# Output rows four to a partition in an attention and gated-convolution kernel, stored as 112 and 15 partitions

## The chip, the cores and the metric

The kernel runs on one core of a Trainium2 chip. The metric is the device time of one execution in microseconds. The engines are named as in the profile: PE (TensorE matmul), PEld (TensorE weight load, the loading of the matmul's stationary operand), DVE (VectorE), ACT (ScalarE), POOL (GpSimd) and SP (SyncE, which issues DMAs). DMAs are issued from the queues of SP and ACT.

## The reference

Two stages, with B = 4, N = 6336 and C = 256, in float32. q and k are normalised over N, the scores are channel by channel, and the result goes through a causal convolution of five taps, a sigmoid and two matrix products:

```python
qn = q / (norm(q, axis=1) + 1e-6);  kn = k / (norm(k, axis=1) + 1e-6)
s = kn.transpose(0, 2, 1) @ qn / tau          # 256 x 256 per batch
a = exp(s - s.max(-1)); a /= a.sum(-1) + 1e-9
x = v @ a                                     # 6336 x 256 per batch
gate_pre = sum(conv_w[k] * xp[:, k:k + S] for k in range(5))   # xp: x with four zero rows ahead
gate = 1 / (1 + exp(-gate_pre))
out = (gate * (x @ w_val)) @ w_out
```

## The kernel before

Per batch there is a score pass and a chunk pass. The score pass reads q and k in 17 groups of up to three rows per partition and accumulates the 256 x 256 scores (`score_group`, matmuls at line 242). Its weights are every second channel of a row (`dealt`: channels are dealt to two halves, so neighbours in a weight load lie two floats apart). Rows with index below `nw` go as plain float32 in one product; the others are split into a high and a low part (`hi`) and go as three faster products. The softmax (`softmax`, a generator run in small steps between other work) turns the scores into the weights `w` of two products: `a`, and `a` times `w_val`.

The chunk pass takes 12 chunks of 508 rows and one of 240 (`chunks`; `all_steps` are the 52 pairs of batch and chunk). For each chunk, v is loaded, transposed by DVE and split (`load_v`, `turn_v`, `cast_v`, `low_v`), then:

- `conv`: x, transposed (channels on partitions), by matmuls at line 401 into `x_ps`, and five taps on ACT and DVE into `gate`;
- `sigmoid`, then `value`: the value product at line 401 into `val_ps`, multiplied into `gate`;
- `split_g`: `gate` into a high and a low part, `g_hi` and `g_lo`, tiles of 128 channels x 2 halves x 508 rows in float32;
- `finish`, run one step later: the output product at line 468. The gate is the stationary operand (its columns are the chunk's rows) and `w_out` the moving one, 256 columns wide. For each block of up to 128 rows six matmuls (two channel halves by three products) accumulate in half a PSUM bank. ACT copies a bank with two blocks to `o_sb` (line 478) and two DMAs store the chunk.

Before the change, block j of a chunk is the rows j x 128 to j x 128 + 127, the last block starting at w - 128, so that it overlaps the one before it by four rows (by 16 in the chunk of 240). Partition p of block j holds row j x 128 + p, so each stored piece is one row of 1 KB.

```python
o_ps[:, u * C:(u + 1) * C], gs[:, h, off:off + P], ws[:, h, :]      # line 468: out, weights, moving
store.dma_start(out=out[b, t0:t0 + full * P].rearrange("(j p) c -> p j c", p=P), in_=o_sb[:, 0:full, :])
```

The stores go out on ACT's queue, those of the last chunk but one on SP's. For the very last chunk `finish` copies its two blocks one by one, on ACT and on DVE, and stores each from its own queue (lines 474 and 476). `o_sb` has two buffers in the pool `w_p`. The tiles of q and k (`raw`) have six buffers in the pool `raw_p`.

The order of the work is written out by hand in the main loop (a step runs score groups, convolution, value product, split and the finish of the step before), with `behind(...)` and `tc.issue_after` for fine places. Within that, the framework's scheduler orders each engine's instructions by a simulated timeline; it also places the waits.

Of the kernel before, what the change touches and what calls it, by code (L numbers as in the profile page):

```python
# [9 lines left out]
F32 = mybir.dt.float32  # L10
# [8 lines left out]
P = 128  # L19
# [11 lines left out]
def kernel(  # L31
# [13 lines left out]
    nc = tc.nc  # L45
    B, N, C = q.shape
# [6 lines left out]
    raw_p = ctx.enter_context(tc.tile_pool(name="raw_p", bufs=6))  # L53
# [5 lines left out]
    w_p = ctx.enter_context(tc.tile_pool(name="w_p", bufs=2))  # L59
# [5 lines left out]
    first = RP % GROUP or GROUP  # L65
# [274 lines left out]
    NT = -(-(HALO + WMAX) // P)  # L340
# [99 lines left out]
    def split_g(b, i):  # L440
# [11 lines left out]
            nc.gpsimd.tensor_tensor(gl[:, :, 0:w], gate[:, :, 0:w], gh[:, :, 0:w].bitcast(F32), ALU.subtract)  # L452
        gts[b, i] = (gh, gl)

    def finish(b, i):
        t0, w = chunks[i]
        gh, gl = gts.pop((b, i))
        nt = -(-w // P)
        offs = [min(j * P, w - P) for j in range(nt)]
        o_sb = w_p.tile([P, NT, C], F32, name="o_sb")  # L460
        for j in range(0, nt, 2):
            pair = offs[j:j + 2]
            o_ps = ps.tile([P, 512], F32, name="o_ps", tag="bank")
            for u, off in enumerate(pair):
                n_ = 0
                for h in range(NH):
                    for gs, ws in ((gh, wo_hi), (gh, wo_lo), (gl, wo_hi)):
                        nc.tensor.matmul(o_ps[:, u * C:(u + 1) * C], gs[:, h, off:off + P], ws[:, h, :],  # L468
                                         start=n_ == 0, stop=n_ == 3 * NH - 1)
                        n_ += 1  # L470
            if (b, i) == all_steps[-1]:

                for u, (copy, dma) in enumerate(((nc.scalar.copy, nc.scalar), (nc.vector.tensor_copy, nc.sync))[:len(pair)]):
                    copy(o_sb[:, j + u, :], o_ps[:, u * C:(u + 1) * C])
                    first = max((j + u) * P - pair[u], 0)
                    dma.dma_start(out=out[b, t0 + pair[u] + first:t0 + pair[u] + P], in_=o_sb[first:P, j + u, :])
                continue
            marks["ACT"] = nc.scalar.copy(o_sb[:, j:j + len(pair), :], o_ps[:, 0:len(pair) * C].rearrange("p (j c) -> p j c", c=C))
        if (b, i) == all_steps[-1]:
            return  # L480
        full = w // P
        store = nc.sync if (b, i) == all_steps[-2] else nc.scalar
        store.dma_start(out=out[b, t0:t0 + full * P].rearrange("(j p) c -> p j c", p=P), in_=o_sb[:, 0:full, :])
        if w % P:
            store.dma_start(out=out[b, t0 + full * P:t0 + w], in_=o_sb[P - w % P:P, full, :])


    all_groups = [(b, g) for b in range(B) for g in range(NG)]
    all_steps = [(b, i) for b in range(B) for i in range(NC)]
# [5 lines left out]
    marks = {}  # L495
# [125 lines left out]
    for n in range(len(all_steps)):  # L621
# [39 lines left out]
        if prev:  # L661
            with behind(*{len(all_steps) - 2: ["CONV"], len(all_steps) - 1: ["G"]}.get(n, [])):
                finish(*prev)
    finish(*all_steps[-1])


# [30 lines left out]
```

## Time and profile before

| | |
|---|---|
| time, three runs | 619.65, 622.12, 622.36 us (median 622.12) |
| profiled execution | 620.85 us, span 619.0 us |
| mean granted TensorE clock | 0.993 |
| PE busy | 599.0 us (97%) |
| DVE, POOL, ACT busy | 498.1, 489.7, 469.3 us |
| output product (line 468) | 1,200 matmuls, 1,200 weight loads |
| stores | 104 DMAs, 50 + 50 of them (lines 483 and 485) on ACT's queue |

A page of the profile gives the busy time of each engine, the span in 40 slices, the DMA queues, the chain of work that ended last, and the costliest groups of instructions. A group's row has its line, engine and operation, what it writes and reads, the count, the busy time, the mean length of one in ns, and the idle time ahead of it with what ended it. Matmuls are pipelined: one of 256 columns is shown as 280 ns long, while the next starts much sooner, so that their pace is to be read from the starts, or from the chain's pieces (start, length, line, count). A weight load overlaps the matmul before it.

### The profile page before, as it was taken

Reading aid. Unit: us, or ns where it says so; the run is one execution under the profiler, and the core shown is the slowest. Engines: PE = TensorE matmul, PEld = TensorE weight load, DVE = VectorE, ACT = ScalarE, POOL = GpSimd, SP = SyncE. Lnnn points to the kernel's source line nnn. Section 1 sums busy time; section 2 is a strip of 40 time slices with the busy share of each in tenths; the row PEclk is TensorE's granted clock in tenths of the full one; section 3 lists DMA queues with packets and bytes.
Section 4 is the critical chain, followed back from the end, with each engine's and each line's share of the span. In section 5 each row is a group of like instructions: output and inputs, shape, how many; then the busy total and the mean of one; then the engine's idle time right before and its main releaser. Section 6 shows DMA issues by size and latency. Waiting matters only on the chain.

```text
span 619.0 us, 10261 instructions
## 1 busy us (share of the span) xinstructions
PE 599.0 (97%) x3596; PEld 537.3 (87%) x3596; DVE 498.1 (80%) x763; ACT 469.3 (76%) x576; POOL 489.7 (79%) x261
## 2 busy tenths in 40 slices
PE   8998999898999999999999999999999999999996
PEld 7987888787898998999989999898898888888895
DVE  3885689778788879889887887988887998988782
ACT  5567868486779896877868987787868876877763
POOL 2776798699787699998986699998986486877842
PEclk9997999999999999999999999999999999999999
DMA  8999996475464666765664767665143245552113
GB/s 278 401 275 320 236 286 189 141 189 177 143 189 143 190 185 176 214 186 151 187 179 140 198 169 219 166 216 136 51 99 106 69 120 135 130 140 83 64 45 116
DMA packets 154596, 105.80 MB, mean 171 GB/s; under 512 B 110768, under 2 KB 137648, under 8 KB 154544
## 3 DMA queue, kind: packets, MB, share of 16 engines
q1 hardware_dynamic: 128768, 79.82, 46.5%
q10 hardware_dynamic: 25776, 25.32, 13.5%
q8 instruction: 28, 0.46, 0.3%
q14 instruction: 24, 0.20, 0.1%
HBM read 79.16 MB, written 25.95 MB: 170 GB/s over the span
## 4 chain that ended last, share of the span: by engine, by line
PE 71%; DMA 12%; ACT 5%; POOL 4%; issue 4%; DVE 2%; SPq 2%; ACTq 0%; POOLq 0%; DVEq 0%
PE o_ps L468 19%; PE val_ps L401 18%; PE x_ps L401 18%; PE s_ps L242 14%; DMA v_raw<-in_v_dram 4%; DMA raw<-in_q_dram 2%; DMA raw<-in_k_dram 2%; DMA out_dram<-o_sb 2%; POOL v_lo L385 2%; DMA w_raw<-in_moe_w_val_dram 1%; PE o_ps L328 1%; DVE gate L421 1%; POOL acc L217 1%; SPq L365 1%; SPq L76 1%
## 5 line engine op out<-in xcount | busy, mean ns | idle before, releaser
L421 DVE SCALAR_TENSOR_TENSOR gate<-x_ps,wa,gate 128x508 f32<-128x508 f32 (+1 forms) x400 | 268.6, 715 | 14.0 <-ACT gate L418 11.3
L385 POOL TENSOR_TENSOR v_lo<-v_raw,v_hi 128x1024 fp32r<-128x1024 f32 (+1 forms) x52 | 123.7, 2380 | 45.0 <-ACT v_hi L379 44.7
L201 POOL TENSOR_TENSOR hi<-raw,hi 128x1536 fp32r<-128x1536 f32 (+3 forms) x51 | 142.5, 2797 | 20.0 <-ACT hi L200 13.5
L401 PE MATMUL x_ps<-v_hi,w 128*128 128x512 f32 (+1 forms) x416 | 140.7, 388 | 5.6 <-DVE gate L421 5.6
L401 PE MATMUL val_ps<-v_hi,w 128*128 128x508 f32 (+1 forms) x416 | 134.2, 382 | 0.0
L452 POOL TENSOR_TENSOR g_lo<-gate,g_hi 128x1016 fp32r<-128x1016 f32 (+1 forms) x50 | 118.6, 2372 | 15.1 <-ACT g_hi L451 12.1
L217 DVE TENSOR_TENSOR acc_ps<-acc_ps,sq 128x512 f32<-128x512 f32 (+1 forms) x124 | 85.8, 692 | 37.8 <-ACT sq L214 35.6
L468 PE MATMUL o_ps<-wo_hi,g_hi 128*128 128x256 f32 x400 | 112.9, 285 | 0.0
L468 PE MATMUL o_ps<-wo_lo,g_hi 128*128 128x256 f32 x400 | 111.4, 281 | 0.0
L214 ACT ACTIVATE sq<-raw 128x1536 f32<-128x1536 f32 (+3 forms) x69 | 96.2, 1396 | 17.4 <-DMA raw<-in_k_dram 14.0
L217 POOL TENSOR_TENSOR acc<-acc,sq 128x512 f32<-128x512 f32 x68 | 88.7, 1305 | 25.6 <-ACT sq L214 24.4
L468 PE MATMUL o_ps<-wo_hi,g_lo 128*128 128x256 f32 x400 | 107.7, 282 | 1.1 <-POOL g_lo L452 1.1
L242 PE MATMUL s_ps<-hi 128*128 128x256 f32 (+1 forms) x714 | 97.7, 286 | 0.0
L401 PEld LDWEIGHTS x_ps<-v_hi,w 128*128 128x128 f32 x416 | 77.1, 188 | 20.1 <-issue 6.2
L242 PEld LDWEIGHTS s_ps<-hi 128*128 128x128 f32 (+1 forms) x714 | 92.1, 196 | 2.5
L401 PEld LDWEIGHTS val_ps<-v_hi,w 128*128 128x128 f32 x416 | 77.1, 188 | 13.5
L373 DVE STREAM_TRANSPOSE v_raw<-v_raw 128x1024 f32<-128x1024 f32 (+1 forms) x52 | 62.3, 1200 | 31.3 <-DMA v_raw<-in_v_dram 27.7
L418 ACT ACTIVATE gate<-x_ps,wa 128x508 f32<-128x508 f32 (+1 forms) x104 | 68.1, 666 | 21.4 <-PE x_ps L401 20.6
L438 DVE TENSOR_TENSOR gate<-val_ps,gate 128x508 f32<-128x508 f32 (+1 forms) x104 | 65.3, 654 | 20.8 <-ACT gate L431 10.5
L242 PE MATMUL s_ps<-raw 128*128 128x256 f32 (+1 forms) x324 | 79.2, 391 | 0.7 <-DMA raw<-in_k_dram 0.7
L401 PE MATMUL x_ps<-v_lo,w 128*128 128x512 f32 (+1 forms) x208 | 79.8, 384 | 0.0
L401 PE MATMUL val_ps<-v_lo,w 128*128 128x508 f32 (+1 forms) x208 | 79.0, 380 | 0.0
(81 smaller groups left out, 811.1 us busy)
## 6 DMA issues: line engine op xcount, KB each, us to landing
raw<-in_q_dram SPq DMA_DIRECT2D x64, 384.0 KB
raw<-in_k_dram SPq DMA_DIRECT2D x64, 384.0 KB
v_raw<-in_v_dram SPq DMA_DIRECT2D x176, 128.0 KB
out_dram<-o_sb ACTq DMA_DIRECT2D x47, 384.0 KB
out_dram<-o_sb ACTq DMA_DIRECT2D x47, 124.0 KB
v_raw<-in_v_dram SPq DMA_DIRECT2D x16, 120.0 KB
v_raw<-in_v_dram SPq DMA_DIRECT2D x16, 64.0 KB
raw<-in_q_dram SPq DMA_DIRECT2D x4, 128.0 KB
```

The source lines that it names most:

```text
L201: marks["POOL"] = nc.gpsimd.tensor_tensor(hi[r, js, :, 1, :], raw[r, js, :, :], hi[r, js, :, 0, :].bitcast(F32), ALU.subtract)
L214: marks["SQ"] = nc.scalar.activation(sq[0:np_, ja:jb], raw[0:np_, ja:jb], AF.Square)
L217: marks["DVE" if key == "acc" else "POOL"] = eng.tensor_tensor(st[key][0:np_], st[key][0:np_], sq[0:np_, j], ALU.add)
L242: marks["PE"] = nc.tensor.matmul(st["s"][:, h, :], lhs, rhs, start=False, stop=stop and h == NH - 1 and n_ == len(ops) - 1)
L373: marks["T"] = nc.vector.transpose(t, t)
L385: nc.gpsimd.tensor_tensor(tl[:, :, 0:g, :], vraw.pop((b, i)), th[:, :, 0:g, :].bitcast(F32), ALU.subtract)
L401: marks["PRODUCT"] = nc.tensor.matmul(ps, wt[:, which, ws, ch, hs], vs[:, ch, lo:hi_], start=n_ == 0, stop=n_ == 3 * NH - 1)
L418: nc.scalar.activation(gate[:, h, 0:w], x_ps[:, 0:w], AF.Copy, scale=cw[:, h, 0:1])
L421: marks["TAP"] = nc.vector.scalar_tensor_tensor(gate[:, h, 0:w], x_ps[:, tap:tap + w], cw[:, h, tap:tap + 1], gate[:, h, 0:w], ALU.mult, A ...
L438: nc.vector.tensor_tensor(gate[:, h, 0:w], val_ps[:, 0:w], gate[:, h, 0:w], ALU.mult)
L452: nc.gpsimd.tensor_tensor(gl[:, :, 0:w], gate[:, :, 0:w], gh[:, :, 0:w].bitcast(F32), ALU.subtract)
L468: nc.tensor.matmul(o_ps[:, u * C:(u + 1) * C], gs[:, h, off:off + P], ws[:, h, :], start=n_ == 0, stop=n_ == 3 * NH - 1)
```

## The change

Row r x nt + j of a chunk now goes to partition r of block j, with nt = 4 blocks (2 in the chunk of 240) of 127 (120) rows. The weights of line 468 are therefore every nt-th float of the gate. A partition's four rows lie one behind the other in the output, so that a stored piece is 4 KB, and blocks no longer overlap. `even` splits a store into the largest multiple of 16 partitions and the rest: 112 and 15, or 112 and 8. The very last chunk's copies go to tiles of the pool `raw_p` under the tag of q and k instead of `o_sb`, and each of its two blocks is stored by two DMAs in pieces of 1 KB.

```diff
+    def even(rows):
+        whole_ = rows // 16 * 16
+        return [x for x in ((0, whole_), (whole_, rows)) if x[0] < x[1]]
+
     def finish(b, i):
         t0, w = chunks[i]
         gh, gl = gts.pop((b, i))
         nt = -(-w // P)
-        offs = [min(j * P, w - P) for j in range(nt)]
-        o_sb = w_p.tile([P, NT, C], F32, name="o_sb")
+        rows = w // nt
+        at_end = (b, i) == all_steps[-1]
+        if not at_end:
+            o_sb = w_p.tile([P, NT, C], F32, name="o_sb")
         for j in range(0, nt, 2):
-            pair = offs[j:j + 2]
+            pair = range(j, min(j + 2, nt))
             o_ps = ps.tile([P, 512], F32, name="o_ps", tag="bank")
-            for u, off in enumerate(pair):
+            for u in range(len(pair)):
                 n_ = 0
                 for h in range(NH):
                     for gs, ws in ((gh, wo_hi), (gh, wo_lo), (gl, wo_hi)):
-                        nc.tensor.matmul(o_ps[:, u * C:(u + 1) * C], gs[:, h, off:off + P], ws[:, h, :],
+                        turn = gs[:, h, 0:w].rearrange("p (r j) -> p j r", j=nt)[:, j + u, :]
+                        nc.tensor.matmul(o_ps[0:rows, u * C:(u + 1) * C], turn, ws[:, h, :],
                                          start=n_ == 0, stop=n_ == 3 * NH - 1)
                         n_ += 1
-            if (b, i) == all_steps[-1]:
+            dst = out[b, t0:t0 + w].rearrange("(r j) c -> r j c", j=nt)
+            if at_end:
                 for u, (copy, dma) in enumerate(((nc.scalar.copy, nc.scalar), (nc.vector.tensor_copy, nc.sync))[:len(pair)]):
-                    copy(o_sb[:, j + u, :], o_ps[:, u * C:(u + 1) * C])
-                    first = max((j + u) * P - pair[u], 0)
-                    dma.dma_start(out=out[b, t0 + pair[u] + first:t0 + pair[u] + P], in_=o_sb[first:P, j + u, :])
+                    o_end = raw_p.tile([P, C], F32, name="o_end", tag="raw")
+                    copy(o_end[0:rows], o_ps[0:rows, u * C:(u + 1) * C])
+                    for r0, r1 in even(rows):
+                        dma.dma_start(out=dst[r0:r1, j + u, :], in_=o_end[r0:r1])
                 continue
-            marks["ACT"] = nc.scalar.copy(o_sb[:, j:j + len(pair), :], ...)
+            marks["ACT"] = nc.scalar.copy(o_sb[0:rows, j:j + len(pair), :], ...)
...
-        full = w // P
         store = nc.sync if (b, i) == all_steps[-2] else nc.scalar
-        store.dma_start(out=out[b, t0:t0 + full * P].rearrange("(j p) c -> p j c", p=P), in_=o_sb[:, 0:full, :])
-        if w % P:
-            store.dma_start(out=out[b, t0 + full * P:t0 + w], in_=o_sb[P - w % P:P, full, :])
+        for r0, r1 in even(rows):
+            store.dma_start(out=dst[r0:r1], in_=o_sb[r0:r1, 0:nt, :])
```

More of the change, by code (lines that the diff above doesn't have):

```diff
@@ L467, in finish @@
                     for gs, ws in ((gh, wo_hi), (gh, wo_lo), (gl, wo_hi)):
-                        nc.tensor.matmul(o_ps[:, u * C:(u + 1) * C], gs[:, h, off:off + P], ws[:, h, :],
+                        turn = gs[:, h, 0:w].rearrange("p (r j) -> p j r", j=nt)[:, j + u, :]
+                        nc.tensor.matmul(o_ps[0:rows, u * C:(u + 1) * C], turn, ws[:, h, :],
                                          start=n_ == 0, stop=n_ == 3 * NH - 1)
                         n_ += 1
-            if (b, i) == all_steps[-1]:
+            dst = out[b, t0:t0 + w].rearrange("(r j) c -> r j c", j=nt)
+            if at_end:
                 for u, (copy, dma) in enumerate(((nc.scalar.copy, nc.scalar), (nc.vector.tensor_copy, nc.sync))[:len(pair)]):
-                    copy(o_sb[:, j + u, :], o_ps[:, u * C:(u + 1) * C])
-                    first = max((j + u) * P - pair[u], 0)
-                    dma.dma_start(out=out[b, t0 + pair[u] + first:t0 + pair[u] + P], in_=o_sb[first:P, j + u, :])
+                    o_end = raw_p.tile([P, C], F32, name="o_end", tag="raw")
+                    copy(o_end[0:rows], o_ps[0:rows, u * C:(u + 1) * C])
+                    for r0, r1 in even(rows):
+                        dma.dma_start(out=dst[r0:r1, j + u, :], in_=o_end[r0:r1])
                 continue
-            marks["ACT"] = nc.scalar.copy(o_sb[:, j:j + len(pair), :], o_ps[:, 0:len(pair) * C].rearrange("p (j c) -> p j c", c=C))
-        if (b, i) == all_steps[-1]:
+            marks["ACT"] = nc.scalar.copy(o_sb[0:rows, j:j + len(pair), :],
+                                          o_ps[0:rows, 0:len(pair) * C].rearrange("p (j c) -> p j c", c=C))
+        if at_end:
             return
-        full = w // P
         store = nc.sync if (b, i) == all_steps[-2] else nc.scalar
-        store.dma_start(out=out[b, t0:t0 + full * P].rearrange("(j p) c -> p j c", p=P), in_=o_sb[:, 0:full, :])
-        if w % P:
-            store.dma_start(out=out[b, t0 + full * P:t0 + w], in_=o_sb[P - w % P:P, full, :])
+        for r0, r1 in even(rows):
+            store.dma_start(out=dst[r0:r1], in_=o_sb[r0:r1, 0:nt, :])
     all_groups = [(b, g) for b in range(B) for g in range(NG)]
```

## The prediction

> **What bounds the kernel now.** I read first the busy shares and the slices of the page, then the stretches.
>
> ```profile
> span 619.0 us, 10261 instructions
> ...
> PE 599.0 (97%) x3596; PEld 537.3 (87%) x3596; DVE 498.1 (80%) x763; ACT 469.3 (76%) x576; POOL 489.7 (79%) x261
> ```
> ```profile
> 95.00:155.00 60.00, 53.25 (x331) 47.67 (x331) 49.31 (x71) 42.89 (x48) 53.83 (x25) 1.00 0.62 171
> 155.00:470.00 315.00, 315.00 (x1987) 285.64 (x1986) 266.67 (x407) 258.28 (x309) 279.04 (x140) 1.00 0.58 166
> 470.00:600.00 130.00, 128.54 (x767) 114.05 (x766) 111.69 (x169) 97.35 (x139) 88.53 (x46) 1.00 0.38 101
> 600.00:619.00 19.00, 13.02 (x101) 12.34 (x99) 5.79 (x12) 8.01 (x14) 4.96 (x3) 0.95 0.30 97
> ```
>
> The columns are span, PE, PEld, DVE, ACT and POOL busy, granted clock, DMA share and GB/s. From 155 to 470 us PE is busy 315.00 of 315.00 us at full clock, then 128.54 of 130. What changes the pace of PE's stream there changes the time one for one; what shortens another engine's work or a transfer changes nothing. Idle PE is left in two places that the change can reach: 6.75 us between 95 and 155, and the tail.
>
> So the question is what sets PE's pace in the output product (line 468), whose stationary operand the change re-reads with a step. The chain of waits gives pitches, the weight-load rows give durations:
>
> ```profile
> 362.89 0.71 PE o_ps L468 x6
> 363.60 1.44 PE s_ps L242 x12
> 365.04 1.34 PE val_ps L401 x12
> 366.38 0.24 PE o_ps L468 x2
> 366.62 1.38 PE x_ps L401 x6
> 368.00 0.23 PE o_ps L468 x2
> 368.24 1.39 PE x_ps L401 x6
> 369.62 2.35 PE o_ps L468 x20
> ```
> ```profile
> L242 PEld LDWEIGHTS s_ps<-hi 128*128 128x128 f32 x702 | 90.4, 196 | 2.1
> ...
> L468 PEld LDWEIGHTS o_ps<-wo_hi,g_hi 128*128 128x128 f32 x400 | 75.3, 188 | 3.6
> ```
>
> The output product runs at 2.35/20 = 117.5 ns a matmul, the score product at 1.44/12 = 120 ns, though both stream 256 columns. They differ in the weights: line 468 reads 128 neighbouring floats, line 242 every second one (`dealt`, a step of 8 bytes), and its load is 8 ns longer. What a load alone takes is seen where matmuls of one column follow each other (line 274, first four from contiguous floats, then four by steps of 8 bytes):
>
> ```profile
> 182.62 0.53 PEld L274 LDWEIGHTS o_ps<-ones,acc_all 128*128 128x128 f32 x4
> ```
> ```profile
> 183.07 0.43 PEld L274 LDWEIGHTS o_ps<-ones,acc_all 128*128 128x128 f32 x3
> ```
>
> Each row is the pitch times one less than the count, plus the last load's own length. That gives (0.53 - 0.19)/3 = 113 ns contiguous and (0.43 - 0.20)/2 = 115 to 118 ns at 8 bytes. So the score product, at 120, goes at its loads' pace, while the output product, at 117.5, is held by its columns with only some 4 ns to spare. **Anything over that 4 ns in a load of line 468 goes into the time.**
>
> **The change part by part.** *Weights by steps of 16 bytes.* With four rows to a partition, `turn` takes every fourth float: 127 of them, 16 bytes apart. It is 3 x 400 loads; in each batch's last chunk (240 wide, two rows to a partition) 2 x 6 of them step 8 bytes, so 1,152 step 16 bytes and 48 step 8. The first matmul of a run behind line 401's products has its load beside a wider one (1.38/6 = 230 ns), which hides it; in the rows above that is 3 of 30. I count 1 in 10 as hidden and 1,037 as exposed.
>
> No row shows a load at 16 bytes. The near end is the 8-byte step: 120 ns, +2.5 ns x 1,037 = +2.6 us; a load that cost nothing more would stay at 117.5. For the far end I ask how fast any reader walks along its partition. ACT has the same pair as PE, a cast from contiguous floats (line 200) and one by 8 bytes (line 379):
>
> ```profile
> L379 ACT CAST v_hi<-v_raw 128x1024 fp32r<-128x1024 f32 x48 | 54.4, 1135 | 7.1 <-PE val_ps L401 5.1 <-DMA v_raw<-in_v_dram 1.7
> ...
> L200 ACT CAST hi<-raw 128x1024 fp32r<-128x1024 f32 x22 | 23.3, 1059 | 0.0
> ...
> L379 ACT CAST v_hi<-v_raw 128x512 fp32r<-128x512 f32 x4 | 2.6, 654 | 1.1 <-PE val_ps L401 1.1
> ```
>
> By 8 bytes ACT takes (1135 - 654)/512 = 0.94 ns an element, 8.5 bytes of partition per ns, and is 7% slower than contiguous. PE's score load walks 128 x 8 bytes in 120 ns, 8.5 per ns, also some per cent slower than contiguous. The output product's moving operand, contiguous, walks 1,024 bytes in 117.5 ns, 8.7 per ns; line 401's six of 512 columns in 1.38 us give 8.9, and the difference between 512 and 256 columns (230 - 117.5 ns for 1,024 bytes) 9.1. No row walks faster than 9.1, and the two readers that would have had to were slowed to 8.5. The new load spans 127 x 16 = 2,032 bytes: 223 ns at 9.1, 239 at 8.5. The far end is +121.5 x 1,037 = +126 us.
>
> I take the walking limit, not the 8-byte row, because a step of 8 bytes is where the slowing begins on two engines, and 16 asks for twice that walk: 222 ns, +104.5 x 1,037 = **+108.4 us**. The 48 loads by 8 bytes add 0.1 us.
>
> [...]
>
> *Stores.* A step's two stores on ACT's queue become two others: 112 and 15 partitions (112 and 8 in the last chunk), each partition 4 KB in one piece instead of 1 KB.
>
> ```profile
> L483 ACTq DMA_DIRECT2D out_dram<-o_sb x50: 351/384/438, 97.9 to 609.7; - x50
> L485 ACTq DMA_DIRECT2D out_dram<-o_sb x50: 276/398/618, 98.3 to 610.1; - x50
> ```
> ```profile
> DMA packets 154596, 105.80 MB, mean 171 GB/s; under 512 B 110768, under 2 KB 137648, under 8 KB 154544
> ...
> q10 hardware_dynamic: 25776, 25.32, 13.5%
> ```
>
> Issues per step stay two, at 384 and 398 ns on a queue whose engine is 76% busy; SP's two of the last step but one stay two. The output's 4 x 6,336 = 25,344 rows of 1 KB become 4 x (12 x 127 + 120) = 6,576 pieces, 6,696 with the very last chunk's 120 written as 240, so packets fall by about 18,600. Cost zero, covered by PE's full busy time above; with that cover gone (95 to 155 us) it could only be a gain, the second rival.
>
> *Copies of 127 rows.* ACT's copies of line 478 keep 512 columns; zero.
>
> *Tail.* The last chunk's copies leave `o_sb` (two buffers) for `raw`'s six, whose readers are long done.
>
> ```profile
> 609.68 0.38 ACTq L483 DMA_DIRECT2D out_dram<-o_sb  x1
> ...
> 610.09 0.41 ACTq L485 DMA_DIRECT2D out_dram<-o_sb  x1
> ...
> 612.75 0.28 PE L468 MATMUL o_ps<-wo_hi,g_lo 128*128 128x256 f32 x1
> 614.28 0.37 ACT L474 COPY o_sb<-o_ps 128x256 f32<-128x256 f32 x1 [2.04 <-DMA out_dram<-o_sb]
> 614.68 0.35 ACTq L476 DMA_DIRECT2D out_dram<-o_sb  x1
> 614.68 0.42 DVE L474 COPY o_sb<-o_ps 128x256 f32<-128x256 f32 x1 [4.30 <-ACT o_sb L474]
> 615.13 0.32 SPq L476 DMA_DIRECT2D out_dram<-o_sb  x1
> ```
>
> Now the ACT copy waits until 614.28 for the stores issued at 609.68 and 610.09. Without that it starts at 612.75 + 0.28 = 613.03, 1.25 us earlier; next late is the last matmul itself. Each queue then issues two stores (112 and 8 partitions) instead of one, +0.32 to 0.35 us before the last lands: -0.9 us net. If the 8-partition piece landed slower than the big one, the gain would be zero.
>
> *Sum.* The profiled execution took 620.85 us, its span 619.0 and 1.85 around it; the median of the runs, 622.12, is 0.2% above. 620.85 + 108.4 + 0.1 - 0.9 = 728.5; I say 728.
>
> **The rivals.**
>
> *Extra per byte skipped.* The 8-byte step skips 4 bytes and costs 2 to 5 ns alone, 7% on ACT; if cost grows with bytes skipped, 12 bytes cost three times that: 6 to 15 ns, or 21% of 113 = 24 ns. Loads of 119 to 137 ns, +1.5 to +19.5 ns x 1,037 = +2 to +20 us: at the upper end 620.85 + 20 - 0.9 = 640. For it: one step only is shown. Against it: ACT's 0.94 ns per 8 bytes fits a limit as well. A limit that is softer than I think, at one and a half times 113 = 170 ns, is +54 us: 674.
>
> *Load no slower than by 8 bytes.* Then 620.85 + 2.6 - 0.9 = 622.5, or 620 if it costs nothing: no change that shows. Under 0.5%, 3.1 us, a measurement of this kernel can't tell. For it: the smallest surcharge that the trace shows is 2 ns. Against it: two engines slow down at the first step that the trace has.
>
> *Faster.* PE's idle 6.75 us of 95 to 155 us lies where the chain runs through stores:
>
> ```profile
> 97.88 2.97 DMA out_dram<-o_sb
> ...
> 133.50 4.74 DMA out_dram<-o_sb
> ```
> ```profile
> PE x_ps L401 <- DVE gate L421: 5.6, 2, 3.0
> ...
> PE o_ps L468 <- POOL g_lo L452: 1.1, 1, 1.1
> ```
>
> If 4 KB pieces land sooner and the work behind them starts sooner, up to 6.75 us return, with the tail 620.85 - 6.75 - 0.9 = 613. It decides only if loads stay under 120 ns and more than 2.2 us of the 6.75 come back (2.2 + 0.9 = 3.1). Against it: PE's own waits there (the second rows: total, times, longest) name a DVE and a POOL result, no store.
>
> **How the numbers follow.** Walking limit 0.42 (point 728; its own range, loads of 210 to 239 ns, 716 to 746); extra per byte or a softer limit 0.20 (625 to 700); load as by 8 bytes 0.31, of which 0.03 lands just over 3.1 us; faster 0.07. Slower by over 0.5%: 0.42 + 0.20 + 0.03 = 0.65; within 0.28; faster 0.07. The forecast is the likeliest case, 728. The range reaches from 618, below the unchanged case, to 742: it leaves out the faster rival and a tenth at the top of the walking limit. Both signs hold much of the chance, which makes it this wide.
>
> **What would show it.** Weight load of line 468: 188 ns now; about 300 by my forecast, 195 to 212 by the extra per byte, at most 196 by the third case. The pieces of 20 output matmuls in the chain: 2.35 us now, about 4.4 by the forecast, 2.40 if nothing happens. Score and value products keep 120 and 230 ns, and PE stays near full, with DVE's share down from 80% to about 68%. DMA packets fall to about 136,000. The last ACT copy starts 0.3 us behind the last matmul, with no wait for a store. The forecast is wrong if line 468's pitch stays under 130 ns.

## The result and the profile after

The changed kernel takes 733.91 us (median of five runs, 732.64 to 734.86) against 621.51 us before: ratio 1.1812, 95% interval 1.1785 to 1.184. It is 18% slower, 6 us over the forecast of 728. All of it stands in one group of instructions. First the page of the changed kernel, busy time of each engine:

```profile
span 732.1 us, 10259 instructions
...
PE 720.1 (98%) x3596; PEld 662.6 (90%) x3596; DVE 503.3 (69%) x763; ACT 474.8 (65%) x576; POOL 489.4 (67%) x261
```

The other engines do the work that they did before, in a longer span. PE's busy time has grown by 121.1 us. The line of the output product is now 476. These are two rows of its weight loads, shapes kept apart (between the two bars stand busy us and mean ns):

```profile
L476 PEld LDWEIGHTS o_ps<-wo_lo,g_hi 128*127 128x127 f32 x384 | 125.0, 326 | 0.2
...
L476 PEld LDWEIGHTS o_ps<-wo_hi,g_hi 128*120 128x120 f32 x16 | 3.0, 190 | 0.2
```

The 127-column loads, by steps of 16 bytes, take 326 ns where 188 stood; the 120-column loads of the last chunks, by 8 bytes, take 190. In the chain of waits (start, length, what):

```profile
526.22 1.37 PE val_ps L401 x6
527.59 0.81 PE o_ps L476 x4
...
528.84 1.38 PE x_ps L401 x6
530.22 4.54 PE o_ps L476 x20
```

A run of 20 output matmuls takes 4.54 us instead of 2.35; line 401 keeps its 1.38 us for six. The run of four shows how: its first load lies beside a wide matmul (the row above it) and is hidden (117 ns), the other three cost 232 ns each, 0.117 + 3 x 0.232 = 0.81. The matmuls of the line, busy time over the whole span, changed kernel first and the kernel before second:

```profile
sum 732.10, PE 285.04 PEld 282.64; mean PE 47.51 PEld 47.11
```
```profile
sum 619.00, PE 163.09 PEld 155.95; mean PE 32.62 PEld 31.19
```

That is +122 us, PE's whole growth. The time grew by less, 113 us in the profiled executions, because PE idles less (732.1 - 720.1 = 12.0 us against 20.0). Most of that idle time went from one stretch (columns as in the prediction's stretches):

```profile
95.00:155.00 60.00, 60.00 (x297) 55.58 (x296) 43.99 (x60) 40.30 (x45) 47.87 (x22) 1.00 0.57 157
```

PE had 53.25 busy us in this stretch and now has 60.00. It gets through fewer matmuls in it (297 against 331), and DVE and POOL, for which it waited there before, have less to do in the same time (43.99 and 47.87 busy us against 49.31 and 53.83). The stores changed as announced, packets and ACT's queue:

```profile
DMA packets 136468, 105.80 MB, mean 145 GB/s; under 512 B 111288, under 2 KB 113064, under 8 KB 136416
...
q10 hardware_dynamic: 8002, 25.32, 11.2%
```

And the tail, by time:

```profile
727.28 0.28 PE L476 MATMUL o_ps<-wo_hi,g_lo 128*120 128x256 f32 x1
727.60 0.37 ACT L484 COPY o_end<-o_ps 120x256 f32<-120x256 f32 x1 [0.84 <-PE o_ps L476]
...
728.45 0.75 SPq L486 DMA_DIRECT2D out_dram<-o_end  x2
```

The copy waits for the last matmul alone (0.04 us behind its end). From there the span has 732.1 - 727.56 = 4.5 us left, where it had 619.0 - 613.03 = 6.0.

### The profile page after: what moved, and what is told of

Its sections match the earlier page's. It is cut to its first block, busy times and chain, and to the rows that moved or that the text cites. A ratio compares the mean times of both kernels' runs of the same rounds, so it can differ in the third digit from the quotient of the medians.

```text
span 732.1 us, 10259 instructions
## 1 busy us (share of the span) xinstructions
PE 720.1 (98%) x3596; PEld 662.6 (90%) x3596; DVE 503.3 (69%) x763; ACT 474.8 (65%) x576; POOL 489.4 (67%) x261
## 4 chain that ended last, share of the span: by engine, by line
PE 89%; DMA 5%; ACT 2%; DVE 1%; SPq 1%; issue 1%; ACTq 0%; DVEq 0%
PE o_ps L476 36%; PE val_ps L401 18%; PE x_ps L401 18%; PE s_ps L242 15%; DMA raw<-in_q_dram 3%; DMA v_raw<-in_v_dram 1%; DMA raw<-in_k_dram 1%; PE o_ps L328 1%; DVE gate L421 1%; SPq L76 1%; ACT sq L214 1%; PE s_ps L248 0%; ACT hi L200 0%; PE o_ps L274 0%; SPq L365 0%
## 5 line engine op out<-in xcount | busy, mean ns | idle before, releaser
L476 PE MATMUL o_ps<-wo_lo,g_hi 128*127 128x256 f32 (+1 forms) x400 | 156.4, 391 | 0.0
L476 PE MATMUL o_ps<-wo_hi,g_hi 128*127 128x256 f32 (+1 forms) x400 | 152.0, 380 | 0.0
L476 PE MATMUL o_ps<-wo_hi,g_lo 128*127 128x256 f32 (+1 forms) x400 | 148.3, 383 | 0.0
L488 ACT COPY o_sb<-o_ps 127x512 f32<-127x512 f32 (+1 forms) x99 | 58.1, 587 | 136.4 <-PE o_ps L476 133.2
L476 PEld LDWEIGHTS o_ps<-wo_hi,g_hi 128*127 128x127 f32 (+1 forms) x400 | 127.5, 319 | 2.6
L476 PEld LDWEIGHTS o_ps<-wo_lo,g_hi 128*127 128x127 f32 (+1 forms) x400 | 128.0, 320 | 0.3
L476 PEld LDWEIGHTS o_ps<-wo_hi,g_lo 128*127 128x127 f32 (+1 forms) x400 | 125.5, 321 | 1.2
```

Of the source, the lines that this page charges most:

```text
L476: nc.tensor.matmul(o_ps[0:rows, u * C:(u + 1) * C], turn, ws[:, h, :], start=n_ == 0, stop=n_ == 3 * NH - 1)
L488: marks["ACT"] = nc.scalar.copy(o_sb[0:rows, j:j + len(pair), :], o_ps[0:rows, 0:len(pair) * C].rearrange("p (j c) -> p j c", c=C))
```

## The experiments

Ratios are to the kernel before, run on the same chip in the same series (its median was 619.6 to 620.1 us there).

**The step alone.** The kernel before with (shortened)

```diff
+ at = h * (w - 4) + j + u
+ turn = gs[:, h, off:off + P] if w < ROWS else gs.rearrange("p h t -> p (h t)")[:, at:at + 4 * P - 3:4]
- nc.tensor.matmul(..., gs[:, h, off:off + P], ws[:, h, :], ...)
+ nc.tensor.matmul(..., turn, ws[:, h, :], ...)
```

> The kernel before, and in the chunks of 508 rows the weights of the output product are read by steps of 16 bytes (128 of them, so that the rows of a chunk land in another order); stores, tail and all else are those of before. Theory, the weight load by 16 bytes: the load's row goes from 188 to about 330 ns, the output product's pitch to about 231 ns, and the time to 733 to 737 us, all of the change's slowdown. Rival, the stores in 112 and 15 partitions or the 127-row matmuls cost something: the time stays clearly under that of the change, at 622 if the load costs nothing.

Measured: 738.6 us, ratio 1.1898 (1.1862 to 1.1934), 1.6 us over the range that I expected. The line's load (the mean has 16 contiguous loads among its 400) and a run of 20:

```profile
L470 PEld LDWEIGHTS o_ps<-wo_hi,g_hi 128*128 128x128 f32 x400 | 128.1, 320 | 2.5
```
```profile
315.95 4.57 PE o_ps L470 x20
```

The step alone makes the whole slowdown; stores, blocks of 127 rows and tail are not needed for it.

**All but the step.** The changed kernel with

```diff
- turn = gs[:, h, 0:w].rearrange("p (r j) -> p j r", j=nt)[:, j + u, :]
+ turn = gs[:, h, (j + u) * rows:(j + u + 1) * rows]
```

> The changed kernel with contiguous weights in the output product (block j is the rows j x 127 and on, so that rows land in another order); stores of 112 and 15 partitions, 4 KB pieces and the new tail stay. Theory: load 188 ns, pitch 117.5 ns, time 619 to 622 us: the stores and the tail are worth between 0 and 2 us. Rival, the stores carry part of the slowdown: over 625 us. Rival, the stores help in the stretch from 95 to 155 us, where PE was idle for 6.75 us before: 613 to 618 us.

Measured: 618.67 us, ratio 0.9976 (0.9955 to 0.9996), 0.3 us under the range that I expected. The load is back at 188 ns:

```profile
L476 PEld LDWEIGHTS o_ps<-wo_hi,g_hi 128*127 128x127 f32 x384 | 72.0, 188 | 3.5
```

The rest of the change is a gain of about 0.24%, just clear of nothing. This kernel and the changed one differ in the step alone, so the step costs 733.91 - 618.67 = 115 us (from two series, in which the kernel before differed by 1.7 us). Put into the kernel before, where the loads have 128 columns instead of 127 and the tail is the old one, it costs 119; how the 4 us between the two part I did not take further. Everything else is worth a little over -1 us. The large gain that the rival hoped for between 95 and 155 us did not come. This kernel's row of that stretch, and the row of the tail-only kernel (below), which has the stores of the kernel before:

```profile
95.00:155.00 60.00, 55.90 (x342) 50.21 (x341) 51.55 (x74) 44.89 (x50) 55.81 (x26) 0.98 0.62 178
```
```profile
95.00:155.00 60.00, 55.88 (x339) 50.21 (x338) 50.55 (x71) 44.66 (x50) 54.16 (x24) 0.97 0.63 173
```

PE idles 4.1 us in both, so that the new stores get no credit for the part that is missing from 6.75.

**Two rows to a partition.** Steps of 8 bytes, pieces of 2 KB:

```diff
- turn = gs[:, h, 0:w].rearrange("p (r j) -> p j r", j=nt)[:, j + u, :]
+ turn = gs[:, h, j * rows:(j + 2) * rows].rearrange("p (r j) -> p j r", j=2)[:, u, :]
- store.dma_start(out=dst[r0:r1], in_=o_sb[r0:r1, 0:nt, :])
+ store.dma_start(out=out[b, t0:t0 + w].rearrange("(k r j) c -> r k (j c)", r=rows, j=2)[r0:r1],
+                 in_=o_sb[r0:r1, 0:nt, :].rearrange("r (k j) c -> r k (j c)", j=2))
```

> The changed kernel with two rows to a partition instead of four: weights by steps of 8 bytes, pieces of 2 KB, the same 112 and 15 partitions and the same tail. It computes all of the reference. Theory (a reader passes over at most about 9 bytes of its partition per ns): 127 x 8 bytes fit beside the matmul, load about 195 ns, pitch 119 to 120 ns, time 621 to 624 us. Rival (any step other than contiguous costs about the double): pitch over 200 ns, time over 700 us.

Measured: 618.39 us, ratio 0.9973 (0.9948 to 0.9997), under the 621 to 624 that I expected.

```profile
L476 PEld LDWEIGHTS o_ps<-wo_hi,g_hi 128*127 128x127 f32 x384 | 75.6, 197 | 3.2
```
```profile
300.29 2.39 PE o_ps L476 x20
```

Load 197 ns, pitch 2.39/20 = 119.5 ns: the 8-byte step costs 2 ns a matmul, not the double. This kernel takes 16% less time than the change. Against the kernel before, 0.27% is hardly clear of nothing, with the interval's end close to 1.

**Steps of 32 and of 12 bytes.** My prediction took the load's price from bytes walked per ns. A longer step tests that. The changed kernel, in the chunks of 508 rows with n = 8, then n = 3 (shortened):

```diff
+ at = (j + u) + 4 * h
+ turn = gs.rearrange("p h t -> p (h t)")[:, at:at + n * (rows - 1) + 1:n]
```

> The changed kernel with the weights of the output product read by steps of 32 bytes in the chunks of 508 rows (127 floats out of both halves of the gate tile, so the products are of other columns); all else as in the change. Theory of the prediction (bytes passed over per ns): 127 x 32 bytes at 8.8 per ns, load about 560 ns, pitch about 460 ns, time about 970 us. Rival (each read that leaves its 16-byte piece costs one further access, and a longer step costs no more): load about 330 ns, pitch about 231 ns, time about 734 us.

Measured: 742.14 us, 8 us over the rival's figure and 228 under the theory's. Load and run:

```profile
L478 PEld LDWEIGHTS o_ps<-wo_hi,g_hi 128*127 128x127 f32 x384 | 127.5, 332 | 2.4
```
```profile
316.32 4.66 PE o_ps L478 x20
```

A pitch of (4.66 - 0.117)/19 = 239 ns: twice the step costs 7 ns more, not 230. The walk along the partition is not the limit; my reason was wrong, though its number for 16 bytes was near (222 ns, measured 232). The expectation for 12 bytes was written with that known:

> The changed kernel with the weights of the output product read by steps of 12 bytes in the chunks of 508 rows (127 floats in a row of steps of three, so the products are of other columns). The 32-byte run has left the theory that each 16-byte piece of the partition costs one access of about 1.8 ns, and that reads that share a piece share the access. Theory, shared pieces: 127 floats by 12 bytes lie in 95 or 96 pieces, 96 x 1.82 = 175 ns, so the output product's pitch is 170 to 185 ns, its load 270 to 285 ns, and the time about 675 to 690 us. Rival, a threshold: any step above 8 bytes costs the double, pitch about 231 ns and time about 734 us. Rival, all is free below 16 bytes: pitch 120 ns, 622 us.

Measured: 672.32 us (one run).

```profile
L478 PEld LDWEIGHTS o_ps<-wo_hi,g_hi 128*127 128x127 f32 x384 | 99.7, 260 | 2.4
```
```profile
318.49 3.52 PE o_ps L478 x20
```

3.52 us for 20 are 117 + 19 x 179 ns. Counting 16-byte pieces that a load touches fits all steps: 127 pieces at 16 bytes and 232 ns give 1.83 ns a piece, 96 pieces at 12 bytes and 179 ns give 1.86, 64 pieces at 8 bytes and 119.5 ns give 1.87, and contiguous floats (32 pieces) stay at 113 to 117.5 ns, where 32 pieces at 1.85 ns would be 59, so that the count does not tell their pace. (At 8 bytes the count, 64 x 1.85 = 118 ns, and the contiguous pitch of 117.5 ns lie within 2 ns of each other, so that the steps of 12, 16 and 32 bytes carry the argument.) At 32 bytes there are 127 pieces again, and the price is nearly the same (239 ns, 1.88 a piece). Shared pieces fit; the threshold (231 ns at 12 bytes) and "free below 16 bytes" (120 ns) fall. The load (260 ns) came out 4% under the range that I had written, the time 3 us.

**The reordering moved to the split.** ACT and POOL read the gate by 16 bytes and write it contiguous (shortened, in a loop over the halves h; PE's weights are contiguous):

```diff
+ turned = gate[:, h, 0:w].rearrange("p (r j) -> p j r", j=nt)
+ high, low = (t[:, h, 0:w].rearrange("p (j r) -> p j r", j=nt) for t in (gh, gl))
+ nc.scalar.copy(high, turned)
+ eng.tensor_tensor(low, turned, high.bitcast(F32), ALU.subtract)
```

> The change with the reordering moved from PE's weights to the split of the gate: ACT and POOL read the gate by steps of 16 bytes and write the high and low parts contiguous, so that PE's weights are contiguous; four rows to a partition, 4 KB pieces and the tail stay. It computes all of the reference. If ACT too takes about 1.8 ns for each 16-byte piece, its cast of 1,016 floats goes from 1.05 to about 2.0 us in all, +1 us a step, which its idle quarter can take; POOL's price is not known, between 2.4 us as now and 4 us. Theory (PE is the bound and its weight load was the only cost): PE's pitch is back at 117.5 ns and the time is 617 to 630 us. Rival (the 16-byte step only moves the loss, since the low part comes late for the output product of the next step): over 640 us with PE waiting for g_lo.

Measured: 631.17 us, ratio 1.0181 (1.0149 to 1.0213), between the two theories. The rows of this kernel, then the contiguous ones of the kernel before:

```profile
L451 POOL TENSOR_TENSOR g_lo<-gate,g_hi 128x508 fp32r<-128x508 f32 x96 | 149.2, 1575 | 18.3 <-ACT g_hi L449 18.1
...
L449 ACT CAST g_hi<-gate 128x508 fp32r<-128x508 f32 x96 | 106.4, 1131 | 12.3 <-DVE gate L438 11.5
```
```profile
L449 POOL TENSOR_TENSOR g_lo<-gate,g_hi 128x508 fp32r<-128x508 f32 x2 | 2.6, 1301 | 0.4 <-ACT g_hi L447 0.4
...
L447 ACT CAST g_hi<-gate 128x508 fp32r<-128x508 f32 x2 | 1.2, 619 | 0.8 <-DVE gate L438 0.8
```
```profile
L451 ACT CAST g_hi<-gate 128x1016 fp32r<-128x1016 f32 x47 | 49.2, 1047 | 16.0 <-DVE gate L438 15.7
```

ACT pays 512 ns more for 508 floats, 1.0 ns each; POOL pays 0.5. Counted in pieces, ACT comes out where PE does. Its contiguous casts of 508 and 1,016 floats (619 and 1047 ns) give 0.84 ns a float and 191 ns besides; without these 191, the 508 floats by 16 bytes take 940 ns, which I estimate as 1.85 ns a piece. So a read by 16 bytes has a price on ACT too, where there is no matmul (1131 ns against 619). 11 us of the slowdown stay. In the profiled execution PE idles 25.4 us (20.0 before) and is busy 606.9 us (599.0); the wait that the rival named, for the low part, is under 1 us of it. How the 11 us part I did not take further.

**Hiding the long load.** In the run of four above the load beside a wide matmul was free (117 ns, against 232 for the three others). The changed kernel with the output matmuls put between the value product's (shortened):

```diff
+ with chained():                       # behind the matmul before it, on PE
      marks["PRODUCT"] = nc.tensor.matmul(ps, wt[...], vs[:, ch, lo:hi_], ...)
+ next(pump[0], None)                   # one output matmul of the step before
```

> The changed kernel, weights still by 16 bytes, with the output product's matmuls of a step put one by one between the value product's 508-column matmuls (from the third step but for the last two). It computes all of the reference. Theory (a load costs only what it outlasts the matmul it lies beside): the long loads of some 220 to 230 ns lie beside matmuls of 227 ns, the contiguous loads of 111 ns beside the output product's, so a pair takes 345 to 352 ns and the time is 620 to 635 us although each load stays at about 330 ns. Rival (a load by 16 bytes takes the memory from the moving operand too, or PE must finish it before anything else): no gain, over 700 us.

Measured: 749.76 us, ratio 1.2096: a miss, slower than the change itself. I had counted 24 partners where the value product of a step has 12. From the chain:

```profile
285.22 0.12 PE o_ps L490
285.34 0.23 PE val_ps L402
285.57 2.91 PE o_ps L490 x13
```

Paired matmuls take 0.12 + 0.23 us, the loads hidden; the other half still runs at 232 ns (12 x 0.232 + 0.117 = 2.90). And the order starved PE: busy 700.3 of 747.4 us, 47 us idle against 12. So the second try used all 24 wide matmuls of a step, and ran the output product two steps behind; beside it went its control with contiguous weights:

> The alternating kernel with partners enough: a step's 24 output matmuls, weights still by 16 bytes, stand one by one between the 24 wide matmuls of the convolution and the value product, and the output product runs two steps behind instead of one, so that its gate is long split (three buffers for g_hi and g_lo, one for o_sb). It computes all of the reference. In the run before, only 12 of a step's 24 had a wide partner: there a pair took 119 + 233 ns, the other half stayed at 231 ns, and PE lost 47 us in waits. Theory (a long load costs only what it outlasts the matmul beside it): a pair takes 352 ns where contiguous loads in the kernel before need 117.5 + 229, so the slowdown of 113 us shrinks to about 6 us plus what the new order costs in waits: 625 to 650 us, and at most 10 us over the control with contiguous weights. Rival (the loads can't be hidden in the whole kernel): over 680 us and far over the control.

> The control of the alternating kernel: the same order, buffers and stores, weights of the output product contiguous (rows land in another order). Theory: 617 to 645 us, which is what the order alone costs; the difference to the alternating kernel with 16-byte steps is the price of the long loads that stay in sight, 0 to 10 us. Rival: as for that kernel, a difference of over 50 us.

Measured: 686.21 us (ratio 1.1065, 1.103 to 1.1099) and, for the control, 670.50 us (1.0785, 1.0705 to 1.0865). The chain of the first:

```profile
400.62 0.24 PE x_ps L402
400.86 0.12 PE o_ps L490
400.98 0.24 PE x_ps L402
...
402.49 0.24 PE o_ps L490
402.72 0.11 PE val_ps L402
402.83 0.24 PE o_ps L490
```
```profile
PE x_ps L402 <- DVE gate L425: 30.4, 18, 3.8
```

Beside a matmul of 512 columns the load is free, within the 0.01 us of these rows. Beside one of 240 columns (0.11 us, the last chunk of a batch) it is not: 0.24 us for the output matmul. In the same order, the 16-byte step costs 686.21 - 670.50 = 15.7 us instead of 115, good to some 4 us, since the control's four runs lie between 663.5 and 672.2. PE's busy time says the same, of this kernel first and of the control second:

```profile
PE 639.9 (93%) x3596; PEld 611.5 (89%) x3596; DVE 501.2 (73%) x763; ACT 467.1 (68%) x576; POOL 486.7 (71%) x261
```
```profile
PE 615.4 (92%) x3596; PEld 544.4 (82%) x3596; DVE 500.8 (75%) x763; ACT 466.0 (70%) x576; POOL 487.1 (73%) x261
```

The step adds 24.5 us here, where it added 720.1 - 600.4 = 119.7 us between all-but-the-step and the change. That the price is one of exposure is shown. All three expectations missed: the times by 36 and 25 us, and the difference, of which I expected at most 10. The order itself costs 50 us: PE waits 30 us in total for the taps on DVE (18 waits, the row above; 31 us in the control).

**The tail alone.** The kernel before with its last copies in tiles of the pool of q and k (shortened):

```diff
- copy(o_sb[:, j + u, :], o_ps[:, u * C:(u + 1) * C])
+ o_end = raw_p.tile([P, C], F32, name="o_end", tag="raw")
+ copy(o_end, o_ps[:, u * C:(u + 1) * C])
```

> The kernel before with only the last copies put into tiles of the pool of q and k (one store each, rows and weights as before). Theory: ACT's last copy starts about 0.3 us behind the last matmul instead of 1.5 us, and the span is 1 to 1.3 us shorter, ratio 0.998, which is all of what the stores-only kernel gained. Rival (that gain came from the 4 KB pieces): ratio 1.000, no earlier landing at the end.

Measured: 621.19 us, ratio 1.0021 (0.9996 to 1.0046): no gain. Its copy does start early, but the stretches of its last us (the last two columns are DMA share and GB/s) show the transfers:

```profile
612.42 0.37 ACT L476 COPY o_end<-o_ps 128x256 f32<-128x256 f32 x1 [0.83 <-PE o_ps L469]
```
```profile
614.00:615.00 1.00, 0.00 (x0) 0.00 (x0) 0.00 (x0) 0.00 (x0) 0.00 (x0) 1.00 0.81 143
615.00:616.00 1.00, 0.00 (x0) 0.00 (x0) 0.00 (x0) 0.00 (x0) 0.00 (x0) 1.00 0.53 123
616.00:617.00 1.00, 0.00 (x0) 0.00 (x0) 0.00 (x0) 0.00 (x0) 0.00 (x0) 0.77 0.26 92
```

With all-but-the-step, where the pieces are 4 KB:

```profile
614.00:615.00 1.00, 0.00 (x0) 0.00 (x0) 0.00 (x0) 0.00 (x0) 0.00 (x0) 1.00 0.55 174
615.00:616.00 1.00, 0.00 (x0) 0.00 (x0) 0.00 (x0) 0.00 (x0) 0.00 (x0) 1.00 0.00 0
```

With 1 KB pieces the transfers still run between 616 and 617, 4 us behind the last matmul's end at 612.39, though the first copy starts 0.03 us behind it instead of 1.25. With the change's stores they are done by 615, 3 us behind the last matmul's end at 611.92; from 614 to 615 the DMA engines move 174 GB/s at a share of 0.55, against 143 at 0.81. So the early copy alone brings nothing. What brings the gain beside it is not shown singly: size of the pieces, stores in 112 and 15 partitions and blocks of 127 rows came together, and no run has them with the old tail.

## Why the prediction was right, and where not

- *PE is the bound, and the output product has some 4 ns to spare.* Right: 113 of the 122 us that PE's stream grew went into the time, and line 401 kept its pace.
- *Weights by 16 bytes, +108.4 us.* The forecast had 104.5 ns x 1,037; measured are 232 - 117.5 = 114.5 ns for the exposed ones, and 122 us of busy time, which at that price are some 1,065 loads. The forecast was 11% under that.
- *The reason behind that number was wrong.* "No row walks faster than 9.1 bytes per ns" described all rows of the trace and was not the limit: at 32 bytes the load walks twice as far in nearly the same time. What the runs show is a price of about 1.85 ns for each 16-byte piece that a load touches (1.83 to 1.88 at steps of 8 to 32 bytes); what the memory does at each piece is not shown. Up to a step of 16 bytes the two theories nearly coincide, since a piece in 1.85 ns is 8.6 bytes per ns; that is why the number held, and it was luck as far as the reason goes: by 32 bytes the same reasoning gave 970 us, where 742 were measured. Nor does the number of columns alone give a load's time: rows of 127 columns took 188 ns contiguous, and 197, 260, 326 and 332 ns by steps of 8, 12, 16 and 32 bytes.
- *Extra per byte skipped (0.20).* Out: over contiguous, a step of 12 bytes costs 62 ns, of 16 bytes 114.5, of 32 bytes about 121, which does not grow with the bytes skipped. The softer limit of 170 ns is out at 16 bytes too.
- *Load no slower than by 8 bytes (0.31).* Out for 16 bytes. The two-row kernel shows what that rival described, at 8 bytes: 119.5 ns and no loss.
- *Faster, by the idle time of 95 to 155 us.* Out as told: the 6.75 us did return, but in a kernel whose PE had become slower, and the stores by themselves brought none of it. I left this term out of the sum, and two misses offset each other in the time: PE's stream grew by 122 us and not 108.5, and 8 us of idle time came back. That is why +122 us in PE became +113 in time, 6 over the forecast.
- *Tail, -0.9 us.* The copy starts as forecast, and the span's rest after the last matmul shrinks by 1.4 us. But "next late is the last matmul itself" does not hold for the early copy alone: in the tail-only kernel the transfers under way came next, and the rest grew to 6.5 us.
- *Signs.* Load of line 476 "about 300": 326. Runs of 20 "about 4.4 us": 4.54. DVE "about 68%": 69%. Packets "about 136,000": 136,468.

## What to carry to other kernels

Before putting a rearrangement into a matmul's weights, compare the pitch of that matmul with what its load takes alone: here the two were some 4 ns apart (117.5 and 113 ns), and a slower load was paid for by each matmul that had no wider one beside it (232 ns by 16 bytes; 0.12 us beside one of 512 columns). A step of two floats, which reads two of each 16-byte piece, was nearly free (119.5 ns); a step of four, which reads one, was not. In this kernel a step of 2 gave pieces of 2 KB at no cost that shows, and a step of 4 doubled the time per exposed matmul. And a limit that fits all rows of one trace may still be the wrong one; a run beyond the range of those rows tells it apart.

## What the runs showed of the hardware that I had not expected

- By steps, the pitch of exposed loads fits the 16-byte pieces that they touch, at 1.83 to 1.88 ns each on PE: by 8 bytes 119.5, by 12 bytes 179, by 16 bytes 232, by 32 bytes 239 ns. Contiguous loads, at 113 ns, lie above that count (59 ns). ACT's cast by 16 bytes comes to an estimated 1.85 ns a piece too; POOL pays 0.5 ns a float more than contiguous, half of ACT's 1.0.
- Wide matmuls beside the long loads keep their pace (0.23 to 0.24 us for 508 and 512 columns, where six of 512 took 1.38 us in the kernel before): these rows show no loss from the load beside them.
- An earlier last copy did not by itself end the span earlier: the rest after the last matmul's end is 6.0 us (before) and 618.9 - 612.39 = 6.5 us (early copies, 1 KB pieces) against 4.5 us in the change (early copies, 4 KB pieces, 112 and 15 partitions) and 617.4 - 612.89 = 4.5 us with two rows to a partition (the same with 2 KB pieces). These are single profiled executions.
